# Another written-out order for the opening steps of a fused mLSTM and GELU kernel

## The chip, the core and the metric

The kernel runs on one core of a Trainium2 chip. A core has five engines with a queue of instructions each: TensorE (PE in the profile, with its weight loads as PEld), VectorE (DVE), ScalarE (ACT), GpSimd (POOL) and SyncE (SP, which here only issues DMAs). Each engine works through its own queue in order; across engines there are only waits on semaphores. The metric is the device time of one execution in microseconds (us), lower is better.

## The reference

The first half is an mLSTM cell: for 4 batches and 8 heads a recurrence over 768 positions with a 40 x 40 state `C`, a normalizer `n` and a running maximum `m`. The second half takes the result as 3072 rows of 320 numbers and sends them through two matrix products with an exact GELU between them.

```python
for t in range(S):                                   # S = 768
    m_new = np.maximum(f_gate[:, :, t] + m, i_gate[:, :, t])
    f_stab = np.exp(f_gate[:, :, t] + m - m_new)
    i_stab = np.exp(i_gate[:, :, t] - m_new)
    C = f_stab * C + i_stab * np.einsum('bhd,bhe->bhde', vt, kt)
    n = f_stab * n + i_stab * kt
    h_tilde, nq = np.einsum('bhde,bhe->bhd', C, qt), (n . qt)
    y[:, :, t] = sigmoid(o_gate[:, :, t]) * h_tilde / np.maximum(np.abs(nq), 1.0)
x = y.transpose(0, 2, 1, 3).reshape(3072, 320)
h = x @ w_in                                         # 320 x 2048
out = (0.5 * h * (1.0 + erf(h / sqrt(2)))) @ w_out   # 2048 x 320
```

## The kernel before

**Chunks.** The 768 positions are cut into six chunks of 128. Inside a chunk the recurrence becomes matrix work on one batch at a time: scores of queries and keys, a mask of exponentials, products with the values, and one update of the carried state. When the four batches of a chunk are done, its 512 rows of `x` go through the "up" product (to 2048, then GELU) and the "down" product. While chunk c goes up and down, the cell steps of chunk c + 1 are woven between its matmuls.

**Two written-out orders.** The kernel doesn't leave the weaving to a scheduler. Two strings of words, `FRONT` (line 27) and `DOWN` (line 36), list the steps; `play` (line 1091) walks a string and runs the step of each word's letter. Each step issues its instructions at the end of the queues of all the engines that it uses, so the order of the words is the order in every queue, SP's and POOL's included. `FRONT` covers everything from the first load up to the end of chunk 0's down product: both the cell steps of chunk 0 (small letters) and those of chunk 1 (capitals).

**The letters of FRONT.** The digit behind a letter is the batch, or for `P`, `L`, `O`, `B` the piece or the running number of chunk and batch.

| word | step (line) | PE | ACT | DVE | other |
|---|---|---|---|---|---|
| `w` `W` | weights (444): exponentials of the mask; for chunk 0 first 10 matmuls into a bank `pm` | `w` only | 8 exps | - | `W0`, `W1` also issue a load of 512 KB |
| `M` | mask (436) | - | - | - | 1 on POOL |
| `g` `G` | sigmoid of the output gate (469) | - | 1 | - | - |
| `t` `T` | turn (505): transposes of keys and queries | 8 transposes | 2 copies | `T`: `vw` | - |
| `s` `S` | scores (527) | 16 records | - | 2 | - |
| `c` `C` | carry (563): the state | 16 or 32 records | `c`: 2 copies | `c`: `vw`; `C`: 4 | - |
| `v` `V` | values (645) | 32 or 64 records | - | `V`: 1 | - |
| `y` `Y` | finish (665): divide, gate | - | - | 5, and a copy `y_rest` | - |
| `x` `X` | turn_y (686): rows of x to columns | 3 transposes | 1 copy | - | `X`: loads for chunk 2 |
| `R` | split_x (712) | - | - | 2 | - |
| `K` | conv_one (369): first half of converting one weight piece | - | 2 | - | - |
| `J` | conv_two (381): second half; fetches piece i + 4 | - | - | 2 | 1 or 2 DMAs |
| `A` `U` | up steps of chunk 0, 4 each (816): `A` for batches 0 and 1, `U` for 2 and 3 | 24 records | 2 GELUs | - | - |
| `F` | 16 rows of chunk 0's down product (1035) | 8 records | last: 4 copies | - | last: 4 DMAs |
| `Z` | split_weight (743) for chunk 1's up product | - | 1 | 1 | - |
| `I`, `k` | idle matmuls (390, 223): `k n` are n of them at once, `I n` are put at the head of the next step's bank | n | - | - | - |
| `E` `N` `D` `d` `Q` `q` | gates of chunks 1 and of 2 to 5, and their decays (265 to 326) | few | 2 exps in `E`, 2 in `N` | scans | `E`, `N`: store M |
| `P` `L` `O` `B` `e` `r` `p` | fetch piece; loads of q and k; of v and o; of M; of chunk 2's blocks; exchange of halves through DRAM | - | - | - | SP's DMAs |

The weights of both products come as pairs of 32-bit words of double width, in 26 pieces: 0 to 9 are `w_in`, 10 to 25 are `w_out`. A piece is fetched into one of four buffers `bits` (line 361), made into `sig` and `pow` on ACT (`K`; two buffers each, lines 374 and 375) and joined on DVE (`J`, lines 385 and 386). Pieces are converted in their order, whatever the order in which they are fetched. `A` number 0 needs pieces 0, 1, 2; number 1 needs 2, 3, 4; number 2 needs 5, 6, 7; number 3 needs 7, 8, 9; `F` number f needs piece 10 + f.

**The banks of an up step.** An `A` or `U` word puts its step aside, and two steps in a row are issued together; any other word issues one that waits alone (`first_up`, line 824). The steps alternate between two pairs of PSUM banks, tags "a" and "b" of the pool `ps_mm`, which the scores `s` (and `S0`, `S2`) and the masks `pm` share. A step can't start before the GELUs of the last user of its pair (line 814) have read it. The banks "tr" of another pool serve `t`, `T`, the gates, `S1`, `S3` and `X`; the banks "h" serve `v`, `c`, `V`, `C`.

**Tables of ACT.** Exponentials, sigmoids and GELUs each need an `ACT_TABLE_LOAD` when the last table used was another one; copies and the two operations of `K` need none.

Of the kernel before, what the change touches and what calls it, by code (L numbers as in the profile page):

```python
# [24 lines left out]


FRONT = """
    I2 O0 g0 L0 P0 L1 E k1 t0 P1 P2 w0 k7 N k2 w1 O1 K L2 Q s0 O3 w2 q D
    k2 d P3 t1 w3 c0 L3 J v0 t2 K K y0 s1 I7 v1 I8 O2 J g1 L4 I5 c1 K I1
    I2 y1 s2 x0 t3 B4 O4 B5 g2 J x1 s3 v2 c2 L5 y2 H T0 x2 G0 v3 g3 c3 K y3  # L30
    M1 J L6 J A x3 M0 K W0 O7 K A O6 O5 J M2 W1 S0 C0 K J J T1 U U
    K L7 V0 K T2 r J J A G2 K G1 Y0 W2 S1 K M3 C1 A J S2 J K W3 K
    V1 C2 Y1 T3 J J U U S3 V2 K K J G3 J Y2 C3 X0 K V3 J K F J F
    K K B8 F J K F F J K F F F R0 X1 J J K F J F K X2 F J
    K F J Y3 K F R1 e J F Z B9 B10 F X3 R2 Z R3 F p"""
DOWN = """
    M0 F Z F L3 W0 M1 Z W1 S0 C0 F F h0 Q2 F K2 G1 D3 B3 Z V0 G2 M2 W2 M3 W3 V1 K3 Q3 F G0 S2 Z Y0 G3 C2 h2 F
    F Y1 X0 V2 V3 F N F j R0 Y2 Y3 X1 F F X2 R1 F R2 X3 R3 F"""
# [1156 lines left out]
```

## Time and profile before

| | |
|---|---|
| median of 3 runs | 463.09 us (462.23 to 463.59) |
| profiled execution | 462.86 us, span 460.7 us |
| granted TensorE clock | 1.00 |
| busy: PE, PEld | 451.9 us (98%), 402.0 us (87%) |
| busy: DVE, ACT, POOL | 308.7, 243.7, 76.7 us |
| first matmul of `A` number 0 (weight load) | 40.13 us |
| first matmul of chunk 0's down product | 91.69 us |
| end of FRONT: first matmul of chunk 1's up product | 127.33 us |

Times in the trace count from the start of the span. The span is 2.2 us shorter than the time of the same execution, and that execution is 0.2 us below the median. Matmuls are recorded with modelled ends, so a busy PE can hide short gaps; where PE really waits is read from the starts of its instructions and from the chain of work that ended last. A matmul in fp32 leaves two records.

### The profile page before, as it was taken

The numbers are of one execution on the slowest core, as the hardware profiler recorded it, in microseconds if no ns is written. First come the engines' busy times: TensorE is split into PE (matmuls) and PEld (weight loads), VectorE is DVE, ScalarE is ACT, GpSimd is POOL, SyncE is SP. The second block draws the span as 40 slices with busy tenths as digits, with TensorE's granted clock in tenths as the row PEclk, the third lists the DMA queues.
The fourth block names the chain that finished last, engine by engine and source line by source line (L and its number), as shares of the span: only waits on it lengthen the run. The fifth ranks groups of instructions, "written<-read, shape, count | busy, mean of one in ns | idle before, by whom it ended". The sixth has DMA issues, their size and how long they took to land.

```text
span 460.7 us, 13113 instructions
## 1 busy us (share of the span) xinstructions
PE 451.9 (98%) x5432; PEld 402.0 (87%) x5432; DVE 308.7 (67%) x661; ACT 243.7 (53%) x541; POOL 76.7 (17%) x117
## 2 busy tenths in 40 slices
PE   9999999999999998999999999999999999999996
PEld 8787888877788898998899998899998899988996
DVE  8677457573579987755578754578654577699950
ACT  7886999953244593113494113395113395257701
POOL 3001030000010432200542200542300422100000
PEclk9999999999999999999999999999999999999999
DMA  7999962295857655219945219853018950200001
GB/s 168 221 221 223 232 177 69 82 242 125 166 129 158 113 96 98 57 51 182 167 79 103 59 57 184 154 92 46 3 57 168 172 94 15 80 35 1 1 0 58
DMA packets 174875, 51.12 MB, mean 111 GB/s; under 512 B 154752, under 2 KB 168352, under 8 KB 174816
## 3 DMA queue, kind: packets, MB, share of 16 engines
q1 hardware_dynamic: 174496, 49.95, 51.0%
q8 instruction: 43, 0.70, 0.6%
q10 hardware_dynamic: 320, 0.33, 0.2%
q14 instruction: 16, 0.13, 0.1%
HBM read 45.47 MB, written 10.03 MB: 120 GB/s over the span
## 4 chain that ended last, share of the span: by engine, by line
PE 95%; DVE 2%; issue 1%; DMA 1%; ACT 1%; SPq 0%; DVEq 0%
PE po L1063 26%; PE pu L947 23%; PE po L1042 8%; PE pu L804 6%; PE pu L958 6%; PE po L917 6%; PE ph L655 4%; PE ps L553 3%; PE pu L810 2%; PE ps L537 2%; PE px L695 2%; PE pf L608 2%; PE pt L515 1%; PE cold L226 1%; PE pf L619 1%; PE pf L575 1%
## 5 line engine op out<-in xcount | busy, mean ns | idle before, releaser
L1063 PE MATMUL po<-w_out,g 128*128 128x160 f32 x512 | 74.4, 302 | 0.0
L962 ACT ACTIVATE g<-pu 128x512 f32<-128x512 f32 x64 | 32.2, 618 | 77.4 <-PE pu L958 77.4
L1063 PEld LDWEIGHTS po<-w_out,g 128*128 128x128 f32 x512 | 70.1, 190 | 1.9 <-ACT g L962 1.3
L947 PE MATMUL pu<-x_hi,w_in_hi 128*128 128x512 f32 x160 | 39.0, 387 | 0.0
L465 ACT ACTIVATE W<-W,aT 128x128 f32<-128x128 f32 x128 | 38.7, 387 | 0.1
L947 PE MATMUL pu<-x_lo,w_in_lo 128*128 128x512 f32 x160 | 37.8, 379 | 0.0
L1063 PE MATMUL po<-w_sums,sums 128*128 128x160 f32 x256 | 36.9, 302 | 0.0
L439 POOL TENSOR_SCALAR_AFFINE_SELECT W<-W 128x1024 f32<-128x1024 f32 (+2 forms) x20 | 24.1, 1209 | 75.8 <-DMA W<-M_d 66.8
L1063 PEld LDWEIGHTS po<-w_sums,sums 128*128 128x128 f32 x256 | 35.0, 190 | 0.4
L1042 PE MATMUL po<-w_out,g 128*128 128x320 f32 x128 | 35.2, 433 | 0.0
L947 PEld LDWEIGHTS pu<-x_hi,w_in_hi 128*128 128x128 f32 x160 | 29.5, 189 | 5.7 <-ACT g L962 1.3
L947 PEld LDWEIGHTS pu<-x_lo,w_in_lo 128*128 128x128 f32 x160 | 30.2, 189 | 4.3
L1042 PEld LDWEIGHTS po<-w_out,g 128*128 128x128 f32 x128 | 24.0, 190 | 9.6
L524 POOL TENSOR_TENSOR vw<-vb,ewT 128x328 f32<-128x328 f32 x12 | 8.7, 737 | 138.5 <-DMA vb<-in_v_dram 55.9
L947 PE MATMUL pu<-x_all,w_mid 128*128 128x512 f32 x80 | 30.3, 379 | 0.0
L947 PE MATMUL pu<-x_all,w_in_mid 128*128 128x512 f32 x80 | 30.3, 379 | 0.0
L559 DVE TENSOR_TENSOR W<-ps,W 128x256 f32<-128x256 f32 (+1 forms) x48 | 18.1, 416 | 17.0 <-PE ps L553 7.1
L804 PE MATMUL pu<-first_x,w_in 128*128 128x256 f32 x128 | 28.8, 381 | 0.0
L804 PEld LDWEIGHTS pu<-first_x,w_in 128*128 128x128 f32 x128 | 23.8, 190 | 3.1
L791 DVE TENSOR_TENSOR sums<-g 128x512 f32<-128x512 f32 x16 | 12.3, 770 | 19.6 <-ACT g L962 19.6
L763 DVE TENSOR_TENSOR w_in_mid<-w_in_hi,w_in_lo 128x512 fp32r<-128x512 f32 x20 | 13.7, 686 | 16.5 <-PE pu L947 16.5
L385 DVE SCALAR_TENSOR_TENSOR pow<-sig,pow 128x320 uint32<-128x320 uint32 (+1 forms) x26 | 14.6, 563 | 13.7 <-ACT pow L375 13.7
(195 smaller groups left out, 917.5 us busy)
## 6 DMA issues: line engine op xcount, KB each, us to landing
W<-M_d SPq DMA_DIRECT2D x16, 512.0 KB, 5.4
bits<-in_moe_w_in_dram SPq DMA_DIRECT2D x20, 256.0 KB, 4.5
bits<-in_moe_w_out_dram SPq DMA_DIRECT2D x16, 320.0 KB, 3.2
blocks<-kq_d SPq DMA_DIRECT2D x32, 128.0 KB, 3.6
ob<-in_o_gate_dram SPq DMA_DIRECT2D x24, 160.0 KB, 3.9
out_dram<-o_sb SPq DMA_DIRECT2D x36, 80.0 KB, 2.0
kq_d<-in_k_dram SPq DMA_DIRECT2D x32, 80.0 KB, 2.5
kq_d<-in_q_dram SPq DMA_DIRECT2D x32, 80.0 KB, 2.5
```

The costliest lines, as they stand in the source:

```text
L385: nc.vector.scalar_tensor_tensor(out=p, in0=s, scalar=3, in1=p, op0=OP.logical_shift_left, op1=OP.bitwise_or)
L439: nc.gpsimd.affine_select(out=x, in_=x, compare_op=OP.is_ge, fill=1.0e30, base=base, pattern=[[0, H], [1, x.shape[2]]], channel_multiplier=-1)
L465: nc.scalar.activation(out=W[n][:, h, :], in_=src, func=AF.Exp, scale=-1.0, bias=aT[:, self.c, r:r + 1])
L559: nc.vector.tensor_tensor(out=w[r, :, t], in0=ps[i][hip][r, :, t], in1=w[r, :, t], op=OP.mult)
L655: nc.tensor.matmul(ph[r, h, :], Pm[:, h, r], vb[turn_of(n)][:, h, :], start=True, stop=True)
L804: nc.tensor.matmul(banks[-1][e][:, i - i0, :], in_tile(i, x)[:, e, i % 2 * P:(i % 2 + 1) * P], first_x[:, x, t0:t1], start=(x == 0 and i = ...
L917: nc.tensor.matmul(in_pairs(po[t]), x[:, t * L:(t + 1) * L], in_turns(w), start=(f, k) == first, stop=(f, k) == last, skip_group_check=True)
L947: nc.tensor.matmul(in_pairs(pus[i][e]), w[k][:, e, i * P:(i + 1) * P], in_turns(x[:, k, :]), start=(n == 0 and k == 0), stop=False, skip_g ...
L958: nc.tensor.matmul(in_pairs(pu[e]), w[r, i // 2, i % 2 * P:(i % 2 + 1) * P], in_turns(x[r, NX, :]), start=False, stop=(n == 2), skip_group ...
L962: nc.scalar.activation(out=g.t[:, HF * e + i, :], in_=pu[e], func=AF.Gelu, scale=4097.0)
L1042: nc.tensor.matmul(po[b], g.t[:, f, b * L:(b + 1) * L], w_out[:, f, :], start=(f == 0), stop=(f == NF - 1))
L1063: nc.tensor.matmul(bank[k][:, t, :], lhs(j, t), rhs(j), start=(first and t == 0 and j == 0), stop=(t == 1 and j == HF - 1), skip_group_che ...
```

## The change

The string `FRONT` is replaced by another order of the same words. The steps themselves and `DOWN` are unchanged. The number of idle matmuls is nearly so: `k` has 12 in both; of the `I` words, of which the last one ahead of a step counts, 16 take effect before and 17 after. In the compiled program ACT loads a table 14 times up to the GELUs of the last two `U` steps before, and 16 times after.

```diff
 FRONT = """
-    I2 O0 g0 L0 P0 L1 E k1 t0 P1 P2 w0 k7 N k2 w1 O1 K L2 Q s0 O3 w2 q D
-    k2 d P3 t1 w3 c0 L3 J v0 t2 K K y0 s1 I7 v1 I8 O2 J g1 L4 I5 c1 K I1
-    I2 y1 s2 x0 t3 B4 O4 B5 g2 J x1 s3 v2 c2 L5 y2 H T0 x2 G0 v3 g3 c3 K y3
-    M1 J L6 J A x3 M0 K W0 O7 K A O6 O5 J M2 W1 S0 C0 K J J T1 U U
-    K L7 V0 K T2 r J J A G2 K G1 Y0 W2 S1 K M3 C1 A J S2 J K W3 K
-    V1 C2 Y1 T3 J J U U S3 V2 K K J G3 J Y2 C3 X0 K V3 J K F J F
-    K K B8 F J K F F J K F F F R0 X1 J J K F J F K X2 F J
-    K F J Y3 K F R1 e J F Z B9 B10 F X3 R2 Z R3 F p"""
+    O0 L0 k3 I4 g0 P0 I3 L1 E P1 k1 O1 I4 t0 P2 w0 k8 K N I2 w1 s0 Q w2 J v0 L2 I2 O3 D q K K t1 w3 c0 L3 t2
+    P3 g1 K O2 y0 L4 J s1 I4 s2 v1 y1 I5 d x0 O4 g2 t3 g3 x1 c1 B4 v2 K c2 B5 J y2 s3 T0 v3 K c3 M1 M0 J L5 x2
+    A y3 L6 J H x3 O7 O6 W0 A M2 J S0 K O5 C0 K J W1 J G0 K J V0 T1 G2 U U K J T2 K W2 Y0 A S1 G1 J L7 C1 A K
+    K S2 M3 V1 J C2 W3 Z J T3 Y1 K U U V2 S3 J K K C3 K X0 K J J J J V3 K J Y2 K F J K F F J R0 G3 K F X1 F B8
+    F X2 F F K F F J K F J Z e Y3 J K J r R1 F X3 K F J F F R2 B9 R3 B10 p F"""
```

## The prediction

> **What bounds the kernel now.** First the page's busy row and its 40 slices:
>
> ```profile
> PE 451.9 (98%) x5432; PEld 402.0 (87%) x5432; DVE 308.7 (67%) x661; ACT 243.7 (53%) x541; POOL 76.7 (17%) x117
> ...
> PE   9999999999999998999999999999999999999996
> ...
> ACT  7886999953244593113494113395113395257701
> ```
>
> PE is busy throughout; ACT is full only from 46 to 92 us (slices 5 to 8), inside FRONT. Then the busy times by stretches of 10 us (PE, PEld, DVE, ACT, POOL, then clock, DMA share, GB/s):
>
> ```profile
> 10.00:20.00 10.00, 8.88 (x87) 7.26 (x85) 7.14 (x22) 8.55 (x29) 0.00 (x0) 1.00 1.02 201
> 30.00:40.00 10.00, 9.04 (x157) 7.96 (x156) 7.42 (x18) 6.70 (x16) 0.36 (x1) 1.00 0.97 238
> 50.00:60.00 10.00, 10.00 (x90) 8.68 (x88) 3.87 (x8) 9.94 (x22) 1.09 (x1) 1.00 0.88 219
> 70.00:80.00 10.00, 10.00 (x159) 8.70 (x154) 7.27 (x19) 9.94 (x21) 0.00 (x0) 1.00 0.24 69
> 100.00:110.00 10.00, 10.00 (x40) 7.12 (x39) 1.47 (x5) 1.56 (x4) 0.00 (x0) 1.00 0.54 139
> ```
>
> Up to 40 us PE has gaps of about 1 us in 10, DMA is full, and part of PE's work is idle matmuls. From 40 to 92 us PE has no gap, but ACT has none to speak of either. From 92 to 127 us (the F rows) DVE and ACT have room. The chain of work that ended last confirms it; at its end the starts of the L804 groups are the up steps:
>
> ```profile
> 40.20 3.65 PE pu L804 x16
> ...
> 62.60 1.02 PE pt L515 x8
> 63.63 3.46 PE pu L804 x16
> ...
> 91.69 17.42 PE po L1042 x64
> ```
>
> From 40 us it holds PE alone, one group starting where the last ended: FRONT's end is the sum of PE's work plus its waits, and an order can change only the waits. Last, the timeline of ACT and PE about `A` number 2 (A2):
>
> ```profile
> 60.95 1.28 ACT L814 ACT_TABLE_LOAD   x1
> 62.25 2.06 ACT L814 ACTIVATE g<-pu 128x512 f32<-128x512 f32 x4
> ...
> 63.36 3.32 PEld L804 LDWEIGHTS pu<-first_x,w_in 128*128 128x128 f32 x16
> ```
>
> A2 reuses the banks of the first U step, so it needs the first of these GELUs (62.87 with its 618 ns). It came at 63.36, so ACT was ahead by only 0.5 us.
>
> **The change part by part.** All times are of the profiled execution (462.86, span 460.7); differences then go onto the median, 463.09.
>
> *The opening, to A0's start at 40.13.* PE's work is the same but for one more idle matmul, two records of 0.13. I laid the steps in their new order with durations and delays from the rows. `k3` now stands ahead of `E`: 18 idle records after 5.79 instead of 12 (which ran to 7.64; the next came at 0.11 to 0.13 each), so E's transpose moves from 7.64 to 8.40 and all gate work of VectorE behind it by 0.76. The copy of `N`'s decays, 13.64 to 14.31 before, ends at 15.42; its exp is followed at 15.95 by W1's exps on ACT. From there ACT is the pacemaker: w1 2.0, w2 2.02, K1 and K2 2.58, t1's copies 0.95, w3 2.1, two state copies 0.55, t2's copies 1.07. Sum 11.27, so s2 can start at 27.25. PE waits for little until then that would matter: w2 for a bank of w1 (0.6), t1 for DVE's copies (0.45), s2's idle matmuls for W1's scores (0.75), s2 for qT (0.3). From s2 to A0 PE has 11.6: s2, s3 1.09 each, v1, v2, v3 1.06 each, T0 1.0, t3 0.95, three `c` 0.6 each, three `x` 0.35 each, I5 1.3, d 0.15. Two waits come on top: c2's bank for state copies that stand behind x0, g2, t3, g3 and x1 on ACT (0.55), and v3 for s3's products on DVE (0.45). A0 starts at 27.25 + 12.6 = 39.85, against 40.13: -0.3. Ends: without the two waits -1.3; with as much again +0.7. I take -0.3, the rows' own sum.
>
> *A0 to A2, where two table loads and a sigmoid are put in.* Count from the end of A0 (before: 44.85). PE: x3 0.27, A1 4.41, S0 1.20, C0 1.19, U0 and U1 9.03, T1 0.83, T2 0.83, V0 0.75, that is 18.51. ACT, from the first GELU 0.10 later to the first of U0: A0's GELUs 0.97, x3 0.36, five loads 6.50, W0's and W1's exps 4.92, A1's GELUs 0.97, K6, K7, K8 3.76, two sigmoids 0.83, T1's copies 0.94, one GELU 0.62: 19.87. So U0's bank is free at 19.97 and A2 starts at 20.0, 1.5 later than PE could. The sum for the old order by the same rows (four loads, no sigmoid) is 17.2 up to the GELUs; the trace has 17.30. Ends: 1.0, if PE itself comes 0.5 later (V0 waits up to 0.2 for S0's products); 2.5, if K7 or K8 each wait 0.5 for a free buffer. I take 1.5.
>
> Each load is a row of 1283 ns, and from 60.95 to 62.25 the whole switch is 1.30. [...]
>
> *A2 to the F rows.* PE from A2's start to F0 is 28.2 with no wait in the sum. The second pair of extra loads (G1 between the GELUs of A2 and A3, 1.30 + 0.47 + 1.30) falls behind A2's GELUs, which S2's banks need: ACT done at 30.56, PE there at 31.1. Cover 0.5; if gone, the shortfall goes on the path. The last U GELUs end at 46.1, F0 needs them at 48.2. Nothing, therefore; ends 0 and +1.
>
> *J and K.* All of `J`'s 52 passes stay; a late one hits the up steps first. J4 ends at about 43, A1 needs it at 44.9; J9 (K9 at 22.4 on the count above) at 23.7, A3 starts at 26.5; C1 and U wait for nothing of DVE. DVE has 2 to 6 of 10 us free there. Nothing; 0.5 if J9 loses its cover.
>
> *SP, POOL, DMA.* Piece 3 is now fetched behind piece 4 and seven loads. With 160 KB per 0.75, 256 KB per 1.15 us (the slices' 220 GB/s) it lands at 27.2; K3 gets to it at 28.9 (cover 1.7, then ACT waits). `O4` (a load of ob) waits on SP for x0 at 31.2, with both loads of M behind it: they land by 38.5 (39.58 before, from the trace), the POOL masks (1.09 each) end by 42, W0's exps need one at 47. `O7` waits for x3, as before. L7 stands behind piece 14, which waits for K10; it has 5 us. `r` and the fetch of piece 25 move back in the F stage, behind loads that wait for X2; needed 15 us later. Nothing; a lost cover would cost ACT up to 1.
>
> *F rows and after.* 34.7 of PE's work plus three `X` either way. F0 to F8 find their pieces converted (J18 is ahead of F0), X3 and R1 come earlier than before, R2 and R3 end 4 us ahead of their use. `DOWN` is unchanged. Nothing; ends -0.5 and +0.5.
>
> Sum: -0.3 + 1.5 = +1.2, so 463.09 + 1.2 = 464.3 us.
>
> **The rivals.**
> 1. *ScalarE's wait is longer.* `K` needs a buffer that DVE's `J` two pieces earlier frees, and ACT stops behind it. In the old order one wait of 0.47 is left on ACT from 45 to 89 us, which speaks against; for it speaks that A2's and S2's margins of 0.5 are used up. With 0.5 at four conversions ahead of A2, and 0.5 at S2 and again at F0: 464.3 + 3 = 467.3. It decides if ACT frees U0's bank later than 21.5 after A0.
> 2. *Faster: the opening's new waits don't come.* The six waits above are 3.1 in all. If banks and copies are ready each time, A0 starts at 36.8 and the time is 463.09 - 3.4 + 1.5 = 461.2. It speaks for it that PE has 3 us of gaps up to 40 us and the new order puts s0 ahead of `Q`, which waited 0.7; against it, that ACT's 11.27 alone pin s2. It decides if A0 starts before 37.2.
> 3. *No change.* PE's work is the same, so the time is the same if A2's wait only uses up what the opening gains: 463.1. For it the span's 98%; against it ACT's 9.94 of 10.
> 4. *Switches cost more than their 1.30.* If the two added ones cost twice that, 2.6 on top: 466.9. The rows above speak against it. [...]
>
> **How the numbers follow.** 0.3% is 1.4 us, about what a measurement can tell from no change. My case has 0.54, with a range of its own from 463.4 to 465.8; of that 0.32 lies within 0.3% and 0.22 above. Rival 1 has 0.22, rival 2 0.16, rival 3 0.06, rival 4 0.02. Slower: 0.22 + 0.22 + 0.02 = 0.46; same: 0.32 + 0.06 = 0.38; faster: 0.16. The range reaches to rivals 1 and 2 and leaves out their further halves: 461.2 to 467.3.
>
> **What would show it.** In the new profile: E's transpose at 8.4; s2 at 27.3 behind ACT's qT; A0 at 39.9; 16 loads up to the last U GELUs; a PE gap of 1.5 ahead of A2, ended by ACT's GELU; F0 at 92.9; the next product (L944) at 128.5; unchanged lengths after it. I am wrong if A2 doesn't wait, if A0 is off by over 1 us, if S2 or F0 waits too, or if a conversion or a DMA ends a wait of PE after 40 us.

## The result, and the profile after

The new order takes 463.89 us (median; 462.99 to 464.48), beside 462.39 us for the old one on the same chip. The ratio is 1.0029, with a 95% interval of 1.0018 to 1.0039, which is 1.3 us (0.8 to 1.8). The prediction was +1.2 us and 464.3. The profiled execution took 463.89 us with a span of 461.7; the granted clock is 1.00.

The page of the new kernel, its busy row and two of its 40 slices:

```profile
PE 451.9 (98%) x5434; PEld 401.6 (87%) x5434; DVE 309.3 (67%) x661; ACT 245.9 (53%) x543; POOL 76.8 (17%) x117
...
PE   9989999999999998999999999999999999999996
...
ACT  6987999873144593113494113494113395157701
```

PE's busy time is the same to the tenth. ACT has 2.2 us more and two more instructions, the two table loads. Its work has spread a little: slices 5 to 7 are still full, slice 8 has gone from 9 to 8 tenths and slice 9 from 5 to 7. Three of the stretches of 10 us shown before (PE, PEld, DVE, ACT, POOL, clock, DMA share, GB/s):

```profile
30.00:40.00 10.00, 9.51 (x163) 8.60 (x162) 9.04 (x25) 6.81 (x16) 1.19 (x1) 1.00 1.00 275
50.00:60.00 10.00, 9.86 (x128) 8.46 (x126) 4.94 (x10) 9.93 (x20) 1.09 (x1) 1.00 0.93 233
100.00:110.00 10.00, 10.00 (x43) 7.13 (x42) 6.90 (x19) 7.32 (x15) 0.00 (x0) 1.00 0.95 232
```

From 100 to 110 us DVE and ACT now have 6.90 and 7.32 us of work instead of 1.47 and 1.56: conversions were put off into the F rows, where there was room, and PE is at 10.00 there as before. The chain of work that ended last, in order of time (start, length, engine, tile, line, number); the lines are three lower in the new file:

```profile
39.08 3.46 PE pu L801 x16
...
61.82 1.28 ACT L811
63.11 0.61 ACT g L811
63.76 3.72 PE pu L801 x16
...
92.28 8.81 PE po L1039 x32
...
127.92 10.36 PE pu L944 x48
```

In the old kernel the chain held PE alone from 40 us on. Now A0 is followed in it by ACT up to a table load and the first GELU of U0, right ahead of the group that is A2. Between, the profile puts the time from 45.10 to 50.66 down to SP and a DMA and that from 52.53 to 55.28 to VectorE, but ACT has no idle time in either. The timeline there, first ACT, then PE's weight loads:

```profile
57.50 1.28 ACT L468 ACT_TABLE_LOAD   x1
58.80 0.47 ACT L468 ACTIVATE ob<-ob 128x320 f32<-128x320 f32 x1
...
61.31 0.48 ACT L468 ACTIVATE ob<-ob 128x320 f32<-128x320 f32 x1
61.82 1.28 ACT L811 ACT_TABLE_LOAD   x1
63.11 2.06 ACT L811 ACTIVATE g<-pu 128x512 f32<-128x512 f32 x4
```

```profile
63.76 3.32 PEld L801 LDWEIGHTS pu<-first_x,w_in 128*128 128x128 f32 x16 [1.34 <-ACT g L811]
```

The load at 57.50 and the two sigmoids of `G0` and `G2` are what the new order puts between W1's exponentials and U0's GELUs. ACT has no idle time from 44.60 to 65.17, and PE idles 1.34 us until it delivers.

Milestones of the two profiles, by the first weight load of each:

| | before | after | difference |
|---|---|---|---|
| A0 | 40.13 | 38.81 | -1.32 |
| A2 | 63.36 | 63.76 | +0.40 |
| F0 | 91.61 | 92.21 | +0.60 |
| chunk 1's up product | 126.89 | 127.49 | +0.60 |
| end of span | 460.74 | 461.73 | +0.99 |

Read alone, this pair says: the opening gains 1.3, the middle loses 1.9, and 0.4 comes later. The experiments show that of these only the middle number can be taken from one pair of profiles.

### The profile page after: what moved, and what is told of

It reads as the page before. It is cut to its first block, busy times and chain, and to the rows that moved or that the text cites. A ratio compares the mean times of both kernels' runs of the same rounds, so it can differ in the third digit from the quotient of the medians.

```text
span 461.7 us, 13117 instructions
## 1 busy us (share of the span) xinstructions
PE 451.9 (98%) x5434; PEld 401.6 (87%) x5434; DVE 309.3 (67%) x661; ACT 245.9 (53%) x543; POOL 76.8 (17%) x117
## 4 chain that ended last, share of the span: by engine, by line
PE 91%; ACT 4%; DVE 2%; DMA 1%; issue 1%; SPq 0%; DVEq 0%
PE po L1060 26%; PE pu L944 23%; PE po L1039 8%; PE pu L955 6%; PE po L914 6%; PE pu L801 4%; PE ph L652 4%; PE ps L550 3%; PE pf L605 2%; PE px L692 2%; PE cold L223 2%; PE ps L534 1%; PE pt L512 1%; PE pu L807 1%; PE pf L616 1%; ACT W L462 1%
## 5 line engine op out<-in xcount | busy, mean ns | idle before, releaser
L1060 PE MATMUL po<-w_out,g 128*128 128x160 f32 x512 | 74.4, 302 | 0.0
L1060 PEld LDWEIGHTS po<-w_out,g 128*128 128x128 f32 x512 | 70.1, 190 | 1.9 <-ACT g L959 1.3
L1060 PE MATMUL po<-w_sums,sums 128*128 128x160 f32 x256 | 36.9, 302 | 0.0
L1060 PEld LDWEIGHTS po<-w_sums,sums 128*128 128x128 f32 x256 | 35.0, 190 | 0.4
```

The lines of the kernel that those rows point to most:

```text
L1060: nc.tensor.matmul(bank[k][:, t, :], lhs(j, t), rhs(j), start=(first and t == 0 and j == 0), stop=(t == 1 and j == HF - 1), skip_group_che ...
```

## The experiments

The theory was that the difference is two terms, a gain up to A0 and ScalarE's wait ahead of A2, the latter made by the added table loads. Rivals were ScalarE's total of work, the order of its other steps, and something behind FRONT. All ratios below are to the old kernel on the same chip, with 95% intervals. The experiments ran on three chips (h and e; b and x; c), so a comparison between groups is one of two such ratios. "Behind E" means behind the start of E's second transpose.

### h1: the new opening with the old middle

```diff
-    L5 x2 A y3 L6 J H x3 O7 O6 W0 A M2 J S0 K O5 C0 K J W1 J G0 K J V0 T1 G2 U U K J T2 K W2 Y0 A S1 G1
+    L5 x2 H G0 y3 L6 J A x3 W0 O7 K A O6 O5 J M2 W1 S0 C0 K J J T1 U U K L7 V0 K T2 r J J A G2 K G1 Y0
...
```

(`H` only opens the buffers of later steps and issues no instruction. `G0 y3 L6 J` stand ahead of `A`, as in the old order.)

> The new order's words up to the first A, then the words of the old order. Theory (two separate terms: the opening gains 1.3 us at A number 0, the middle loses 1.7 through ScalarE's wait ahead of A2): A0 at 38.8, no wait of PE ahead of A2, A2 at 62.0 (old 63.36 - 1.3), F0 at 90.4, time 1.3 us below the old kernel. Rival (ScalarE's total of work from 46 to 92 us sets the end, and an earlier start of PE only makes it wait there): A0 at 38.8, but PE waits for GELUs ahead of A2 by about 0.8 (the cover of 0.5 against the 1.3), time only 0.5 below the old kernel. Rival (the difference sits behind FRONT): the time is that of the new kernel.

Measured: ratio 0.9995 (0.9983 to 1.0008), 461.87 us: 0.2 us below the old kernel, with an interval from 0.8 below to 0.4 above. In its profile (span 460.2) A0 is at 39.16, A2 at 62.45, F0 at 90.70. The table load and the GELUs follow W1's exponentials, K's and T1's work directly:

```profile
58.63 0.58 ACT L515 COPY qT<-pt 128x512 f32<-128x512 f32 x1
59.23 1.28 ACT L811 ACT_TABLE_LOAD   x1
60.53 2.07 ACT L811 ACTIVATE g<-pu 128x512 f32<-128x512 f32 x4
```

A2's weight load follows T2's without a wait:

```profile
62.01 0.47 PEld L512 LDWEIGHTS pt<-ident,qb 128*128 128x128 f32 x4
62.45 3.32 PEld L801 LDWEIGHTS pu<-first_x,w_in 128*128 128x128 f32 x16
```

PE comes earlier than in the old kernel and still doesn't wait for ScalarE. So the new kernel's loss lies in the words of the middle: the new kernel against h1 is 1.0029 / 0.9995 = 1.0034, or 1.6 us. The gain of the opening is smaller in the time than A0's 1.3 us had promised; that led to the question behind b1 to c2.

One thing besides the table loads differs in h1: the new opening has six `K` ahead of A0 and the old one five, so only two are left in h1 between A0 and U0, where both the old and the new kernel have three. That gives ScalarE 1.2 us more room ahead of A2 than the old kernel had. So h1 shows that the opening's gain isn't lost again at A2, but not by itself that the loads made the wait; e1 and e2 leave the number of `K` in this stretch as it was.

### h2: the old opening with the new middle

```diff
-    c3 K y3 M1 J L6 J A x3 M0 K W0 O7 K A O6 O5 J M2 W1 S0 C0 K J J T1 U U
+    c3 K y3 M1 J L6 J K M0 A x3 O7 O6 W0 A M2 J S0 K O5 C0 K J W1 J K J V0 T1 G2 U U
...
```

> The old order's words up to the first A, then the words of the new order. Theory: A0 at 40.1, PE waits about 1.3 ahead of A2 for the first GELU of U0, A2 at 65.0, F0 at 93.4, time 1.7 us above the old kernel and 0.4 above the new one. Rival (ScalarE's queue runs through from the opening, so the wait at A2 depends on the opening): wait ahead of A2 under 0.5, time within 0.5 of the old kernel. Rival (the difference sits behind FRONT): the time is that of the new kernel, A2 no later than in the old one.

Measured: ratio 1.0071 (1.0058 to 1.0084), 465.35 us, 3.3 above the old kernel; the expectation was 1.7. Two of PE's waits in its profile:

```profile
48.32 1.59 PEld L801 LDWEIGHTS pu<-first_x,w_in 128*128 128x128 f32 x8 [1.71 <-ACT first_x L697]
...
66.55 1.59 PEld L801 LDWEIGHTS pu<-first_x,w_in 128*128 128x128 f32 x8 [1.34 <-ACT g L811]
```

The wait ahead of A2 is the predicted one. That it is the same 1.34 as in the new kernel, although only `G2` is in the way here and not `G0`, is chance: from x3's copy to U0's first GELU ScalarE takes 18.11 here and 18.51 in the new kernel, one sigmoid less, and PE, which this copy held up in A1, stands 0.4 nearer to A2 at the copy's end. The other 1.71 is a fault of the seam. A `K` came to stand between the old opening and A0, ScalarE waited 2.48 ahead of it, and x3's copy (47.79) and with it A1 came late. What h2 says of the opening is therefore spoilt.

### e1: the two sigmoids out of the way

```diff
-    v3 K c3 M1 M0 J L5 x2 A
+    v3 K c3 G0 M1 M0 J L5 x2 A
...
-    W1 J G0 K J V0 T1 G2 U U K J T2 K W2 Y0 A S1 G1 J
+    W1 J K J V0 T1 U U K J T2 K W2 Y0 A S1 G1 G2 J
```

> The new order with only two words moved: G0 behind c3 (beside the other sigmoids of the opening) and G2 behind G1. That takes two table loads (1.28 us each) and the sigmoids G0 and G2 from ScalarE's work between W1's exponentials and U0's GELUs. Theory: the wait of 1.34 ahead of A2 goes, A2 at 62.1 to 62.4 (new 63.76), F0 at 90.6 to 91.0, time 1.2 to 1.6 us below the new kernel and so about even with or up to 1.3 below the old one. Rival (the wait belongs to the order of K, W and T1 on ScalarE, not to the loads): A2 waits for 0.8 or more, time within 0.6 of the new kernel. A2's G group then holds two sigmoids behind its GELUs; if S2 or A3 wait for that, 0.4 of the gain is lost.

Measured: ratio 1.0005 (0.9990 to 1.0020), 462.6 us; against the new kernel 1.0005 / 1.0029, 1.1 us faster, a little less than the 1.2 expected at least. The wait ahead of A2 is gone from the profile:

```profile
47.51 1.59 PEld L801 LDWEIGHTS pu<-first_x,w_in 128*128 128x128 f32 x8 [1.11 <-ACT first_x L697]
...
63.92 0.47 PEld L512 LDWEIGHTS pt<-ident,qb 128*128 128x128 f32 x4
64.36 3.32 PEld L801 LDWEIGHTS pu<-first_x,w_in 128*128 128x128 f32 x16
```

A2's weight load follows T2's without a gap. From x3's copy to U0's first GELU ScalarE takes 16.33 us instead of 18.51: one table load (not two, as the expectation has it) and two sigmoids less. PE came 1.11 late in A1 here, but x1, which has no such wait, has none ahead of A2 either. So the load and the two sigmoids made the wait. The profile itself still has F0 at 92.81, no better than the new kernel, for two other reasons: its E stood at 8.64, and A1 waited 1.11 for x3's copy. The first led to b1, the second to x1.

### e2: one sigmoid put into the old order

```diff
-    T0 x2 G0 v3 g3 c3 K y3 M1 J L6 J A x3 M0 K W0 O7 K A O6 O5 J M2 W1 S0 C0
+    T0 x2 v3 g3 c3 K y3 M1 J L6 J A x3 M0 K W0 O7 K A O6 O5 J M2 W1 G0 S0 C0
```

> The old order with only G0 moved, from behind x2 to behind W1: a sigmoid table load, the sigmoid, and the exponentials' or GELUs' table again stand between W1's exponentials and U0's GELUs. Theory (the loads make the wait): ScalarE is 1.28 + 0.42 = 1.7 later at U0's first GELU if W1 is the last user of the exponentials' table ahead of the GELUs (A1's GELUs come first or not decides whether it is one load or two, 1.7 or 3.0), less a cover of 0.5: A2 waits 1.2 to 2.5, the time is 1.2 to 2.5 above the old kernel. Rival (loads are hidden in idle time of ScalarE): time within 0.4 of the old kernel.

Measured: ratio 1.0034 (1.0020 to 1.0047), 463.89 us, 1.6 above the old kernel. One word moved costs as much as the new order's whole middle does. ACT, then PE:

```profile
58.61 1.28 ACT L468 ACT_TABLE_LOAD   x1
```

```profile
64.51 3.32 PEld L801 LDWEIGHTS pu<-first_x,w_in 128*128 128x128 f32 x16 [0.82 <-ACT g L811]
```

The wait ahead of A2 is below the 1.2 expected at least, because PE had waited 0.60 in A1 before, for a conversion, of the kind that x1 looks into. ScalarE has no idle time from A0's first GELU to U0's, so it sets A2's start with or without that wait: 0.82 + 0.60 is 1.42 of this execution's 1.64 from A0 to F0. Some 0.2 more lies in S2's records.

### b1: the idle matmuls k3 moved from ahead of E to behind it

The step of the prediction on E can't be read from one profile. Three profiles show it, each with the idle records and E's transpose behind them (start, length, engine, line, tiles, number). The new kernel:

```profile
5.44 2.08 PEld L223 LDWEIGHTS cold<-w_out 128*128 128x128 f32 x18
7.65 0.13 PEld L249 LDWEIGHTS pg<-ident,a 32*128 32x128 f32 x1
```

e1, with the same opening:

```profile
5.79 2.73 PEld L223 LDWEIGHTS cold<-w_out 128*128 128x128 f32 x18
8.64 0.14 PEld L249 LDWEIGHTS pg<-ident,a 32*128 32x128 f32 x1
```

h2, with the old opening:

```profile
5.29 1.42 PEld L223 LDWEIGHTS cold<-w_out 128*128 128x128 f32 x12
6.82 0.13 PEld L249 LDWEIGHTS pg<-ident,a 32*128 32x128 f32 x1
```

18 records take 2.08 in one and 2.73 in another execution of the same instructions. The starts of single records say why: they come 0.21 apart at first and 0.11 apart from some moment on: by 5.44 in the new kernel, at 7.21 in e1, 4.56 in h2, 6.54 in the old kernel. b1 asks whether the gates behind E carry the six records of `k3` into the time.

```diff
-    O0 L0 k3 I4 g0 P0 I3 L1 E P1 k1 O1 I4 t0
+    O0 L0 I4 g0 P0 I3 L1 E k3 P1 k1 O1 I4 t0
```

> The new order with only the three idle matmuls k3 moved from ahead of E to behind it. So far, every profile with the new opening (the new kernel, h1, e1) has A0 at 31.16 after E's second transpose, and every one with the old opening 32.5 to 32.75; but E's transpose itself stands at 7.65, 7.99, 8.64 in the new and 7.64, 6.82, 7.47 in the old, because the idle records ahead of it run at 0.21 each until a moment between 4.7 and 7.2 us that differs from run to run, then at 0.11. Theory (the six records delay the gates, as the prediction had it, and all behind rides on the gates): E's transpose at 6.8 to 7.7, A0 31.2 behind it, time 0.7 to 1.2 us below the new kernel. Rival (behind E the six records delay PE's own next work by the same amount, and PE's work is the path): A0 at 31.8 to 32.4 behind E, time equal to the new kernel.

Measured: ratio 1.0025 (1.0014 to 1.0036), 463.69 us: the new kernel's time within the expected 0.3. Its profile:

```profile
5.22 1.41 PEld L223 LDWEIGHTS cold<-w_out 128*128 128x128 f32 x12
6.75 0.13 PEld L249 LDWEIGHTS pg<-ident,a 32*128 32x128 f32 x1
6.93 0.97 PEld L223 LDWEIGHTS cold<-w_out 128*128 128x128 f32 x8
```

A0 is at 38.60, 31.85 behind E, where it was 31.16. The rival holds: E is earlier and nothing else is, because the records now stand in front of t0's transposes. They are on the path in either place.

### b2: one idle matmul less

```diff
-    w0 k8 K N I2 w1 s0
+    w0 k7 K N I2 w1 s0
```

> The new order with k7 in place of k8: one idle matmul (two records, 0.22 us) less, so that PE has as many instructions as with the old opening. Question: the fourth of the six chunk stages, from up product to up product, takes 69.96, 70.17 and 69.88 us with the new opening (the new kernel, h1, e1) and 69.19, 69.2 and 69.25 with the old one (the old kernel, h2, e2), through a gap of 0.5 in the state products (L605) that the profile puts down to issue. Theory (the gap hangs on how many instructions stand ahead of it in PE's stream): the gap is gone or elsewhere, that stage takes 69.2, time 0 to 0.8 us below the new kernel. Rival (it hangs on the rotation of buffers or on when DMAs come): the stage keeps its 70.0, time within 0.3 of the new kernel. Ahead of A0 the matmul itself is worth 0 to 0.2.

Measured: ratio 1.0026 (1.0017 to 1.0036), 463.30 us; the fourth stage took 69.71, not 69.2. The theory of the instruction count falls: it is neither 69.2 nor the rival's 70.0 here, and x1 below has 69.29 with as many instructions of PE as the new kernel. The time is within 0.3 of the new kernel's, as the rival has it. The 0.4 us of the milestones' last row need no cause in the change: from chunk 1's up product to the end, where all kernels here run the same instructions, the profiles take 333.9 (old), 333.2 (h2), 333.3 (e2), 334.2 (new), 333.8 (e1), 333.1 (b1), 333.2 (b2) and 334.2 (h1); b3 and x1 below take 333.4 and 333.5, c2 335.0, and c1, whose clock fell there, 336.1. b1 and the new kernel differ in one moved word of the opening and by 1.2 there. What moves it, a gap of 0.5 in the state products (L605) among others, stays open.

### b3: h1 with k3 behind E and k7 for k8

```diff
-    O0 L0 k3 I4 g0 P0 I3 L1 E P1 k1 O1 I4 t0 P2 w0 k8 K N
+    O0 L0 I4 g0 P0 I3 L1 E k3 P1 k1 O1 I4 t0 P2 w0 k7 K N
```

> h1 (new opening, old middle) with k3 behind E and k7 in place of k8: the two terms that gain, without the one that loses. Theory: E's transpose at 6.8 to 7.7, A0 31.2 behind it, no wait ahead of A2, F0 83.0 or less behind E's transpose, time 0.9 to 1.9 us below the old kernel. Rival (the opening isn't bound by the gates): like h1, 0 to 0.5 below the old kernel.

Measured: ratio 0.9988 (0.9977 to 1.0000), 461.66 us, 0.6 below the old kernel. A0 is 31.62 behind E and F0 83.12, not 83.0 or less; the gain over h1 is 0.3, inside the intervals. It sits between the two expectations, as b1's result would have it.

### x1: e1 without two masks

x1 leaves out two masks, so it is a probe and no candidate. In e1's profile, VectorE's two passes of the `J` ahead of A0, GpSimd's masks and ScalarE's next `K`:

```profile
38.70 1.57 DVE L382 SCALAR_TENSOR_TENSOR pow<-sig,pow 128x512 uint32<-128x512 uint32 x1
40.31 1.46 DVE L383 SCALAR_TENSOR_TENSOR w_in<-sig,pow 128x512 uint32<-128x512 uint32 x1
```

```profile
38.30 2.92 POOL L436 TENSOR_SCALAR_AFFINE_SELECT W<-W 128x1024 f32<-128x1024 f32 x2 [33.95 <-DMA W<-M_d]
```

```profile
41.85 0.68 ACT L371 ACTIVATE sig<-bits 128x512 f32<-128x512 f32 x1 [3.46 <-DVE w_in L383]
```

```diff
-    c3 G0 M1 M0 J L5 x2 A
+    c3 G0 J L5 x2 A
```

> e1 without the words M1 and M0: the masks of the first two batches of chunk 1, on GpSimd, are left out. In e1's profile the two VectorE passes of the J ahead of A0 (L382, L383) take 1.57 and 1.46 instead of 0.69 each while those masks run on GpSimd (38.3 to 41.2), ScalarE's next K waits 3.46 for them (1.80 in the new kernel), and PE waits 1.11 for x3's copy in A1. Theory (the masks hold VectorE up): both passes at 0.69, K's wait under 2.0, no wait of PE over 0.5 in A1, time 0.5 to 1.1 us below e1. Rival (the passes are held up by something else, or what they cost is covered in most executions): the passes stay long, or the time is within 0.3 of e1.

Measured: the same passes and the same `K` (line numbers one lower):

```profile
37.82 0.69 DVE L381 SCALAR_TENSOR_TENSOR pow<-sig,pow 128x512 uint32<-128x512 uint32 x1
38.54 0.69 DVE L382 SCALAR_TENSOR_TENSOR w_in<-sig,pow 128x512 uint32<-128x512 uint32 x1
```

```profile
39.31 0.68 ACT L370 ACTIVATE sig<-bits 128x512 f32<-128x512 f32 x1 [1.79 <-DVE w_in L382]
```

No wait of PE over 0.5 is left in A1 or ahead of A2, and A0 to F0 takes 51.92 instead of 53.01. The ratio is 0.9995 (0.9984 to 1.0006) beside e1's 1.0005 (0.9990 to 1.0020): 0.5 us, with intervals that overlap. The masks hold up VectorE: with them the passes took 1.57 and 1.46, without them 0.69 each. What it is worth in the time is not settled. It isn't the same in each execution: of that `J`, both passes are long in e1 and b2, one in h1 and b3, none in the new kernel's profile.

### c1: h1 without k3

```diff
-    O0 L0 k3 I4 g0 P0 I3 L1 E P1 k1
+    O0 L0 I4 g0 P0 I3 L1 E P1 k1
```

> h1 with the three idle matmuls k3 deleted, instead of moved as in b1, where the move changed nothing (A0 31.85 behind E instead of 31.16, A0 itself and the time as in the new kernel). Theory now (in the opening PE's own stream up to t0 and the gates are late alike, so idle records count wherever they stand): A0 31.16 behind E's transpose, and E's transpose itself at 0.7 (six records of 0.11) to 1.3 (of 0.21) less than with k3 for the same moment at which the records get faster; A0 less half that moment at 35.4 to 35.7 (36.02 to 36.35 in all kernels with the new opening and k3); time 0.5 to 1.0 us below h1. Rival (q and k of the first batch, which land at 7.8 to 8.5, set t0, and the idle matmuls are free): A0 less half that moment stays at 36.0 or more, time within 0.3 of h1.

Measured: ratio 0.9988 (0.9979 to 0.9997), 461.97 us, 0.6 below the old kernel; the interval leaves out 1. Its profiled execution (463.85) is slower than its median through a stage behind FRONT, where the granted clock fell, so only its opening is used. The expectation takes half of the moment at which the records get faster off A0, because up to it they come 0.21 us apart and then 0.11. In c1 they get faster at 6.74, E is at 7.72, A0 at 38.88, 31.16 behind E. A0 less half that moment is 35.5, in the range of the theory. Against h1 the time gives 0.3 us, less than the 0.5 to 1.0 expected and inside the intervals. The one trace speaks for the theory; the time can't tell it from the rival.

### c2: h1 without the idle matmuls ahead of s2 and x0

```diff
-    J s1 I4 s2 v1 y1 I5 d x0
+    J s1 s2 v1 y1 d x0
```

> h1 without the idle matmuls of two words: I4 ahead of s2 (eight records, 0.97, behind a wait of 0.97 for VectorE's W) and I5 ahead of x0 (ten records, 1.2). Theory of the prediction (ScalarE's and VectorE's work sets s2, so I4 is nearly free; I5 fills a time in which x0's rows are ready): s2 0.5 earlier, behind qT; x0 1.1 earlier on top; what follows until A0 waits for the state copies of ScalarE and the W of VectorE and gives back up to 1.0; A0 0.6 to 1.6 earlier (34.6 to 35.6 after taking off half the moment of the faster records), time 0.5 to 1.5 us below h1. Rival (all of it is cover for work of other engines): A0 and the time within 0.3 of h1.

Measured: ratio 0.9998 (0.9978 to 1.0019), median 462.14 us, but from 461.57 to 467.09, wider than any other. The profiled execution is the one of 467.09: A0 at 43.20. Two groups of PE's weight loads, and then two stretches (columns as above):

```profile
31.80 0.72 PEld L512 LDWEIGHTS pt<-ident,qk 128*128 128x128 f32 x4 [2.61 <-ACT kT L515]
...
34.30 1.83 PEld L652 LDWEIGHTS ph<-vb,W 128*64 128x64 f32 x32
```

```profile
32.00:36.00 4.00, 4.00 (x55) 3.67 (x54) 0.60 (x1) 2.66 (x7) 0.00 (x0) 0.50 0.84 209
36.00:40.00 4.00, 4.00 (x43) 3.70 (x42) 2.47 (x8) 1.15 (x3) 0.00 (x0) 0.50 0.99 309
```

s2 was earlier, at 25.69 and behind qT as expected (27.05 in h1, whose E stood 0.81 later). Then t3 waited 2.61 for ScalarE's kT, the granted clock fell to 0.50, and v2 took 1.83 for 32 records, which take 1.02 in the new kernel. So this execution can't say where A0 stands at full clock. The median is within 0.2 us of h1's, as the rival has it; the theory's gain of 0.5 to 1.5 doesn't show. Whether the missing idle matmuls have to do with the fall of the clock isn't shown: the other long execution (465.38, mean clock 0.996) has no profile, and c1's, which has both words, shows a clock of 0.50 as well, from 178 to 180 us, behind a wait of PE of 1.49.

## Why the prediction was right

The forecast of +1.2 us met +1.3 (0.8 to 1.8), and the parts behind it mostly hold. Some of the closeness is luck: by the traces below, the opening gains about 0.7 instead of 0.3 and the middle loses 1.9 instead of 1.5, and the two differences cancel.

**A2's wait for ScalarE, +1.5 (1.0 to 2.5).** Right in place, cause and size. The count gave A2 at 20.0 after A0's end; PE's trace has A0's end at 43.53 and A2 at 63.76, 20.2 later. PE could have come 18.51 after A0's end by the sum, and the old kernel did; of the 1.72 more, 1.34 is the idle time ahead of A2 and 0.27 a wait of V0 for S0's products, which the text had put at up to 0.2:

```profile
51.03 0.62 PEld L652 LDWEIGHTS ph<-vb,W 128*32 128x32 f32 x56 [0.27 <-DVE W L537]
```

The check on the old order is off by a little: the same rows give 17.1, not 17.2; the trace has 17.30. e1 takes the wait away by moving two sigmoids, e2 makes one in the old order. The whole stretch from A0 to F0 shows the term best, since it doesn't depend on how the opening went:

| A0 to F0, us | |
|---|---|
| old middle: old kernel, h1, b3, c1, c2 | 51.48, 51.54, 51.50, 51.49, 51.54 |
| new middle: new kernel, b1, b2 | 53.40, 53.43, 54.29 |
| new middle without the wait: e1, x1 | 53.01 (1.11 of it for x3's copy), 51.92 |
| old middle with one sigmoid moved: e2 | 53.12 |
| old opening, new middle: h2 | 55.43 (1.71 of it for x3's copy) |

The new middle costs 1.9 in the trace, and 1.6 in the time (the new kernel against h1). Not all of it is the wait for ScalarE: x1, which has no wait ahead of A2, still takes 0.44 longer than the old middle, 0.22 of it from V0's wait and 0.2 from a gap of PE behind U3 that is told below.

**The opening, -0.3 (-1.3 to +0.7).** The size of this term is what the runs settle least. By the time, h1 gives -0.2 (-0.8 to +0.4). By the traces, A0 stands at 40.13, 39.57 and 39.96 with the old opening, and at 38.81, 39.16, 39.80 and 38.92 with the new one (the new kernel, h1, e1, x1): 0.7 less in the mean. The pair of profiles that the result was first read from has -1.32, because PE's records got faster by 5.44 us in the one and at 6.54 in the other. The prediction said that it would be wrong if A0 were off by over 1 us; A0 was expected at 39.9 and stood at 38.81, so by that sign it was wrong in the profile it named; other profiles with this opening have A0 up to 39.80. E's transpose was expected at 8.4 and stood at 7.65; in e1 it is at 8.64.

A step inside it was mistaken: "all gate work of VectorE behind it by 0.76". E does move, by the six records, which come 0.21 or 0.11 us apart by the moment at which they get faster. But b1 puts E ahead of the records again, and A0 doesn't move with it: it goes from 31.16 to 31.85 behind E. The gates are not what the rest hangs on alone; PE's own records are as late. The prediction counted only one of these two chains and so named the wrong one; it counted the same six records, which is why the size came out close. ScalarE's row of steps up to qT was right (11.07 measured, 11.27 in the sum), but it doesn't set s2: that was expected at 27.25 "behind qT" and stands at 26.70, with qT done at 26.13. Ahead of it stand its idle matmuls, which had waited 0.97 for VectorE's W. Of the six waits priced at 3.1, c2's bank (0.50 measured, 0.55 priced), w2's (0.66, 0.6), the wait for W1's scores (0.97, 0.75), v3's (0.38, 0.45) and one of 0.37 for VectorE's copies ahead of t1 (0.45) are there about as said; s2's own for qT (0.3) is not.

**A2 to F0: nothing.** Right but for 0.2: V2 now follows U2's and U3's last records, behind a gap of 0.33 that S3, first there in the old order, didn't have. A3 to F0 has no wait above that gap, and S2's cover held, with a second pair of loads at 74.39 and 76.17.

**J, K, SP, POOL and DMA: nothing.** Right in the one profile of the new kernel, but for a wrong reason as far as POOL goes. The text priced the masks only as something that W0 waits for, and not by what they do to VectorE beside them. b2, which has the same middle, lost 0.60 in A1 and 0.4 more ahead of A2 with both passes of that `J` at 1.5. Piece 3 was expected 1.7 ahead of K3; ScalarE waited 0.23 for it.

**F rows and after: nothing (-0.5 to +0.5).** Right: F0 to chunk 1's up product takes 35.28 in both kernels, and what follows varies by 1.2 or more in profiles of the same instructions.

**The rivals.** ScalarE's longer wait (467.3) needed U0's bank free later than 21.5 after A0's end; it was free at 20.2. The faster case needed A0 before 37.2; no profile has that. The dearer switches are refuted by a row: from the load's start at 57.50 to the sigmoid's start at 58.80 a whole switch is 1.30, and W1's exponentials ahead of it end at 57.49. In the profiles of the other runs it is 1.29 to 1.37 wherever ACT waits for nothing else behind the load; none shows twice the 1.30, the term of this rival.

**Is anything faster than both?** h1, b3 and c1, the new opening with the old middle, stand at 0.9995, 0.9988 and 0.9988. Only c1's interval (0.9979 to 0.9997) leaves out 1, and 0.6 us is less than the 0.3% that the prediction took as the limit of a measurement. One interval of these three that misses 1 by so little doesn't show that c1 is faster.

## What to carry to other kernels

Where one engine has no idle time over a stretch, count its work up to the next hand-over instead of looking at its share of the span: here a sum of rows from A0's GELU to U0's, with each table load as a row of 1.28 us, gave A2's start to within a quarter of a microsecond. Put operations that share an ACT table next to each other, and into a stretch where ACT waits anyway: e1, with one load of 1.28 us and two sigmoids less between A0's GELUs and U0's, was 1.1 us faster than the new kernel. Don't read a term of one microsecond off the first 10 us of a single pair of profiles: compare stretches that begin behind the start-up, and repeat the rest.

## What the runs showed of the hardware that was not expected

**The moment at which PE gets faster.** The idle records at the start come 0.21 us apart and then 0.11, from a moment that lies at 3.92 us in c2 and at 7.21 in e1, with others between: a spread of 3.3. In these microseconds the profile's clock column reads 1.00 all the same, in the old and in the new kernel. What sets the moment is not shown.

**The clock falls back within a kernel.** In c2's profile waits of 1.17 and 2.61 us within 8 us were followed by a granted clock of 0.50 from 32 to 40 us; in c1's, a wait of 1.49 up to 176.28 by one of 0.50 from 178 to 180, with 6.22 us for 32 records (L1060) that take 4.54 from 184.95 on. In the old kernel's profile a wait of 1.23 at the same step left it at 1.00. Whether idle matmuls bear on it is not shown: of h1's, c1 lacks only `k3`, 170 us earlier.

**A mask on GpSimd and a pass on VectorE at the same time.** A pass of `J` with the inputs `sig` and `pow` takes 0.69 us alone (x1) and 1.57 and 1.46 beside two affine selects (e1). The old kernel has one of 1.46 at 60.74, beside an affine select of 1.56 that began at 60.10; the pass that began at 60.02, just ahead of it, took 0.69. An affine select takes 1.09 alone (old kernel, at 50.59); the two in e1 take 2.92. These rows show no idle time ahead of the long passes: the hold-up across the two engines is no wait on a semaphore, which is all that the text ahead of the prediction counts with. What makes it is not shown.
